# Centroid products as two matmuls in place of three, with the last sum on VectorE

## The chip, the cores and the metric

One core of a Trainium2 chip runs the whole program. The metric is the device time of one execution in microseconds. An execution is timed from outside; the profile's span runs from its first to its last instruction and is a little shorter.

## The reference, cut to what matters

The reference is three layers in a row: attention in which a query sees only the keys of its own cluster, a feed-forward layer with ELU, and a routed layer of eight experts. The change lies in the first. There, for 2 batches x 8 heads, 768 rows and 64 columns:

```
q_n = q / (norm(q) + 1e-06);  k_n likewise;  c_n = centroids / (norm + 1e-06)     # 16 centroids a head
q_assign = argmax(einsum('bhsd,hcd->bhsc', q_n, c_n));  k_assign likewise
mask = q_assign[:, :, :, None] == k_assign[:, :, None, :]
scores = where(mask, q @ k.T / 8, -1e9);  out = softmax(scores) @ v
```

The argmax makes the products with the centroids delicate: two centroids can be nearly as close, so the products are formed in nearly full fp32.

## The kernel before, in words

The attention works through 8 pairs of heads (n = 0 to 7). A pair has 12 units (s = 0 to 11) of 128 queries against 768 keys. A value x that must be exact is held as two fp32r tiles, a head H (x rounded) and a rest L = x - H; a product then is three matmuls, H by H, L by H and H by L.

The steps of a unit are: `scores` (four matmuls of 384 columns into the PSUM tile sA or sB, by turns), `peak` (VectorE takes the row maximum, L402), `exp` (ScalarE, L409), `flip` a and b (six PE transposes, L418, three into the PSUM bank t0 and three into t1), `head` (ScalarE copies a half to ptH, L430), `rest` (VectorE subtracts it to give ptL, L436), `pv` (matmuls with v, L449), and once for two units `pvlow` (ScalarE, L458) and `pvsum` (VectorE, L466). t0 and t1 are one bank each: a flip has to wait until the rest of the flip before it in that bank is done.

Beside these, the next pair is prepared. `similar` (L283, steps simq0, simk0, simq1, simk1, for two halves of 384 tokens) multiplies the centroids with q and k: three matmuls each for q and for k, all six accumulated into partitions 0 to 63 of one PSUM bank, "p". The stationary operand is a window of 64 columns of `cwH` or `cwL`; of its 96 columns only 32 to 63 are not zero, and the window is laid so that q's 32 results land on rows 0 to 31 and k's on rows 32 to 63. `similar_out` (L292, steps sT0 and sT1) copies those 64 rows to SBUF (`rows`) on ScalarE, which frees the bank. `turn_back` (step back) transposes `rows` on the PE, and the steps sv, mx, eqsub, first, least, equal, rows, oT find the argmax and turn it into mask rows. Bank p is used by all steps of this preparation in turn.

Every engine executes its instructions strictly in the order in which the program emits them. That order is written out by hand in `SCHEDULE` (L49), one list for a pair, repeated for each; a plus marks a step for the next pair, a minus one for the pair before. Around the change it reads (L52 to L54, cut):

```
peak2 head0a -head11b -W2 rest0a +simk0 exp2 -W3 -pv5a scores3a +loadqk scores3b +sT0 -rest11b flip1a
peak3 -pv5b flip0b head1a head0b rest1a scores4a exp3 +simq1 rest0b scores4b flip2a peak4 +simk1 head2a vtL
flip1b +sT1 scores5a -pv5c head1b rest2a rest1b exp4 --xH1 scores5b -pv5d --xL1 peak5 loadv flip3a -W4 -W5 -pvlow5 +back
```

Pair 0 is prepared by another list, `START`, ahead of all scores. The constants are built in `first_loads` and `centroids`.

Of the kernel before, what the change touches and what calls it, by code (L numbers as in the profile page):

```python
# [10 lines left out]
F32 = mybir.dt.float32  # L11
F32R = mybir.dt.float32r
# [3 lines left out]
AF = mybir.ActivationFunctionType  # L16
ALU = mybir.AluOpType
# [48 lines left out]
class _Core:  # L66
# [24 lines left out]
    def first_loads(self):  # L91
        nc, c = self.nc, self.const
        V = nc.vector
        cn = self.cn = c.tile([128, 2, 64], F32, name="cn")

        self.load_nat(0, "q")
        nc.scalar.dma_start(out=cn[:, 0, :], in_=self.cent.rearrange("h c d -> (h c) d"))
        self.load_nat(0, "k", nc.scalar)
        self.load_nat(0, "v")
        self.ident = c.tile([128, 128], F32, name="ident")  # L100
        make_identity(nc, self.ident)
        self.ident16 = c.tile([128, 128], BF16, name="ident16")
        V.tensor_copy(self.ident16, self.ident)
        HP = self.H // 2
        self.cwH = c.tile([128, HP, 96], F32R, name="cwH")
        self.cwL = c.tile([128, HP, 96], F32R, name="cwL")
        V.memset(self.cwH.bitcast(F32), 0.0)
        V.memset(self.cwL.bitcast(F32), 0.0)

    def centroids(self):  # L110

        nc, c, cn, HP = self.nc, self.const, self.cn, self.H // 2
        V, S = nc.vector, nc.scalar
        sq = c.tile([128, 64], F32, name="sq")
        V.tensor_tensor(sq, cn[:, 0, :], cn[:, 0, :], ALU.mult)
        t = c.tile([128, 9], F32, name="cnt")
        V.tensor_reduce(t[:, 0:1], sq, axis=AX.X, op=ALU.add)

        S.activation(t[:, 1:2], t[:, 0:1], AF.Sqrt)

        S.activation(t[:, 8:9], t[:, 1:2], AF.Exp, scale=0.0)
        V.tensor_scalar(t[:, 2:3], t[:, 1:2], 1e-30, None, ALU.max)
        V.reciprocal(t[:, 3:4], t[:, 2:3])
        V.tensor_tensor(t[:, 4:5], t[:, 0:1], t[:, 3:4], ALU.mult)
        V.tensor_tensor(t[:, 5:6], t[:, 4:5], t[:, 1:2], ALU.add)
        V.tensor_scalar(t[:, 6:7], t[:, 5:6], 0.5, 1e-6, ALU.mult, ALU.add)
        V.reciprocal(t[:, 7:8], t[:, 6:7])
        V.tensor_scalar(cn[:, 0, :], cn[:, 0, :], t[:, 7:8], None, ALU.mult)
        V.tensor_copy(cn[:, 1, :], cn[:, 0, :])
        pt = self.ps("sA")  # L130
        nc.tensor.transpose(pt[:, 0, 0:128], cn.rearrange("p a d -> p (a d)"), self.ident)
        for j in range(2):
            r = slice(64 * j, 64 * j + 64)
            o = slice(32 + 16 * j, 48 + 16 * j)
            src = pt[r, 0, 0:128].rearrange("p (n j c) -> p n j c", n=HP, j=2)[:, :, j, :]
            V.tensor_copy(self.cwH[r, :, o], src)
            V.tensor_tensor(self.cwL[r, :, o], src, self.cwH[r, :, o].bitcast(F32), ALU.subtract)

    def constants(self):
        nc, c, E = self.nc, self.const, self.E  # L140
# [142 lines left out]
    def similar(self, n, nm, half):  # L283

        p, cs, o = n % (self.H // 2), slice(half * 384, half * 384 + 384), 32 if nm == "q" else 0
        if nm == "q":
            self.sim[n, half] = self.bank_p()
        for j, (w, x) in enumerate(((self.cwH, "H"), (self.cwH, "L"), (self.cwL, "H"))):
            self.nc.tensor.matmul(self.sim[n, half][0:64, 0:384], lhsT=w[:, p, o:o + 64], rhs=self.T[n][nm, x][:, cs],
                                  start=(nm == "q" and j == 0), stop=(nm == "k" and j == 2))  # L290

    def similar_out(self, n, half):  # L292
        self.nc.scalar.activation(self.rows[0:64, half * 384:half * 384 + 384], self.sim.pop((n, half))[0:64, 0:384], AF.Copy)

    def turn_back(self, n):
        ps = self.back[n] = self.bank_p()
# [1087 lines left out]
```

## Time and profile before

| | |
|---|---|
| median of 3 runs | 695.9 us (695.54 to 696.95) |
| profiled execution | 697.57 us, its span 695.8 us |
| mean granted TensorE clock | 0.989 of full speed |
| PE busy | 664.5 us, 96% of the span, 4272 matmuls |
| PEld (weight loads) busy | 606.8 us, 87% |
| VectorE (DVE) busy | 487.7 us, 70% |
| ScalarE (ACT) busy | 448.1 us, 64% |
| GpSimd (POOL) busy | 268.5 us, 39% |

The attention takes about the first third of the span, the feed-forward layer and the experts the rest. Shares of the whole span mix stages with different limits, so the attention has to be read by itself. A pair of heads takes about 30.0 us; step sT0 of the seven pairs after the first starts at 27.26, 57.40, 87.57, 117.56, 147.84, 178.09 and 208.37 us. Busy time counts overlapping instructions once. A PE matmul's duration includes its way through the array; the distance from one start to the next is what it costs in a stream.

### The profile page before, as it was taken

The page shows a single profiled execution, that of the slowest core. Times are in us where ns is not written, and L with a number is a line of the kernel's source. Part 1 is how long each engine was busy: PE and PEld are TensorE (multiplying, and loading weights), DVE is VectorE, ACT ScalarE, POOL GpSimd, SP SyncE. Part 2 cuts the span into 40 slices and gives each one's busy share as a digit, 9 for nine tenths or more (in the row PEclk, how much of TensorE's full clock was granted, in tenths as well). Part 3 has the DMA queues.
Part 4 walks back from the last instruction along what each step waited for, and adds up shares of the span by engine and source line. Part 5 has one row for each costly group of instructions (what it writes and reads, how often), then busy time and mean ns, then how long its engine had stood idle before and what let it go on. Part 6 is the DMA issues. An engine that isn't in the chain of part 4 may idle for free. (4 is left out here: it accounts for less than half of the span.)

```text
span 695.8 us, 12188 instructions
## 1 busy us (share of the span) xinstructions
PE 664.5 (96%) x4272; PEld 606.8 (87%) x4272; DVE 487.7 (70%) x929; ACT 448.1 (64%) x968; POOL 268.5 (39%) x254
## 2 busy tenths in 40 slices
PE   4999999999999988999999999999999998999994
PEld 3799999999998877888888899999999897999994
DVE  5599999999999987999999852432354472226662
ACT  3699989999898986777777664444546321215551
POOL 2323536353455123666788752222242012022010
PEclk9799999999999999999999999999999999999998
DMA  8645757366654623555454355424110259989940
GB/s 175 165 92 130 162 137 163 99 143 140 154 118 118 149 74 107 196 194 192 165 196 161 146 206 210 157 72 145 60 61 16 91 194 374 327 297 315 345 143 13
DMA packets 73670, 111.31 MB, mean 160 GB/s; under 512 B 31073, under 2 KB 41409, under 8 KB 73600
## 3 DMA queue, kind: packets, MB, share of 16 engines
q1 hardware_dynamic: 70400, 106.03, 50.2%
q0 software_dynamic: 1488, 3.99, 1.6%
q8 instruction: 36, 0.59, 0.3%
q10 hardware_dynamic: 1712, 0.43, 0.3%
q14 instruction: 34, 0.28, 0.1%
HBM read 73.81 MB, written 16.92 MB: 130 GB/s over the span
## 5 line engine op out<-in xcount | busy, mean ns | idle before, releaser
L436 DVE TENSOR_TENSOR ptL<-ps_t,ptH 128x384 fp32r<-128x384 f32 x192 | 102.6, 551 | 10.4 <-ACT ptH L430 7.9
L430 ACT ACTIVATE ptH<-ps_t 128x384 fp32r<-128x384 f32 x192 | 91.5, 491 | 17.0 <-PE ps_t L418 13.1
L418 PE MATMUL ps_t<-ident,pe 128*128 128x128 f32 x576 | 94.7, 278 | 2.9 <-DVE ptL L436 2.2
L418 PEld LDWEIGHTS ps_t<-ident,pe 128*128 128x128 f32 x576 | 68.4, 141 | 11.7 <-DVE ptL L436 7.4
L449 PE MATMUL ps_v<-ptH,vt 128*128 128x256 f32 x288 | 78.2, 296 | 0.0
L449 PE MATMUL ps_v<-ptL,vt 128*128 128x256 f32 x288 | 77.2, 296 | 0.0
L697 POOL TENSOR_TENSOR w2L<-r,w2H 128x512 fp32r<-128x512 f32 x28 | 42.4, 1515 | 69.5 <-PE ps_t L742 62.3
L677 POOL TENSOR_TENSOR r<-cv_b,cv_t 128x512 int32<-128x512 int32 x32 | 43.1, 1347 | 44.1 <-DVE cv_b L675 25.5
L449 PEld LDWEIGHTS ps_v<-ptH,vt 128*128 128x128 f32 x288 | 54.0, 189 | 1.6
L449 PEld LDWEIGHTS ps_v<-ptL,vt 128*128 128x128 f32 x288 | 53.5, 190 | 0.2 <-DVE ptL L436 0.2
L725 ACT ACTIVATE e<-ps_p 128x384 f32<-128x384 f32 x32 | 15.7, 491 | 55.4 <-PE ps_p L710 55.4
L402 DVE TENSOR_REDUCE st<-ps_sB 128x1 f32<-128x768 f32 x48 | 45.7, 952 | 4.3 <-PE ps_sB L396 4.2
L402 DVE TENSOR_REDUCE st<-ps_sA 128x1 f32<-128x768 f32 x48 | 45.6, 949 | 4.1 <-PE ps_sA L396 2.9
L1188 POOL DMA_INDIRECT out_dram<-o,dest x10 | 11.5, 1154 | 94.3 <-DVE o L1186 93.7
L728 DVE SCALAR_TENSOR_TENSOR ps_p<-e,ps_p 128x384 f32<-128x384 f32 x32 | 17.9, 559 | 41.1 <-ACT e L726 41.1
L670 DVE SCALAR_TENSOR_TENSOR cv_a<-cv_a,d 128x512 f32<-128x512 f32 x32 | 44.2, 1381 | 3.6 <-ACT cv_a L666 3.4
L697 POOL TENSOR_TENSOR w1L<-r,w1H 128x512 fp32r<-128x512 f32 x32 | 44.1, 1378 | 6.4 <-ACT w1H L696 6.4
L710 PE MATMUL ps_p<-xH,w1H 128*128 128x384 f32 x128 | 44.0, 344 | 2.0 <-DVE gL L731 2.0
L409 ACT ACTIVATE pe<-ps_sA,st 128x768 f32<-128x768 f32 x48 | 43.5, 905 | 0.5 <-DVE st L402 0.5
L409 ACT ACTIVATE pe<-ps_sB,st 128x768 f32<-128x768 f32 x48 | 43.1, 898 | 0.5 <-DVE st L402 0.3
L710 PE MATMUL ps_p<-xL,w1H 128*128 128x384 f32 x128 | 42.9, 335 | 0.0
L710 PE MATMUL ps_v<-xH,w1H 128*128 128x384 f32 x124 | 41.4, 334 | 0.0
(380 smaller groups left out, 1926.3 us busy)
## 6 DMA issues: line engine op xcount, KB each, us to landing
ew<-in_moe_w_dram SPq DMA_DIRECT2D x32, 1024.0 KB
d<-in_moe_w_in_dram SPq DMA_DIRECT2D x16, 512.0 KB
d<-in_moe_w_out_dram SPq DMA_DIRECT2D x16, 512.0 KB
wf_d<-r SPq DMA_DIRECT2D x16, 512.0 KB
r<-wf_d SPq DMA_DIRECT2D x16, 512.0 KB
KA<-kH SPq DMA_DIRECT2D x32, 192.0 KB
natq<-in_q_dram SPq DMA_DIRECT2D x16, 192.0 KB
natv<-in_v_dram SPq DMA_DIRECT2D x16, 192.0 KB
```

What stands on the lines that cost most here:

```text
L402: self.nc.vector.tensor_reduce(st, self.sc[u][:, :, 0:384], axis=AX.XY, op=ALU.max, negate=True)
L409: self.nc.scalar.activation(pe, self.sc.pop(u)[:, :, 0:384], AF.Exp, bias=self.peaks.pop(u), accum_out=self.sums[n][:, s:s + 1])
L418: self.nc.tensor.transpose(ps[:, 0, j * 128:j * 128 + 128], self.pe[u][:, half, j * 128:j * 128 + 128], self.ident)
L430: self.nc.scalar.activation(self.split(u, half)[0], self.tp[u, half][:, 0, 0:384].rearrange("p (c q) -> p c q", c=3), AF.Copy)
L436: self.nc.vector.tensor_tensor(l, self.tp.pop((u, half))[:, 0, 0:384].rearrange("p (c q) -> p c q", c=3), h.bitcast(F32), ALU.subtract)
L449: self.nc.tensor.matmul(self.vp[n, j], lhsT=self.vt[n][:, j // NG, c, :], rhs=t, start=(part == 0 and i == 0), stop=(part == 3 and i == 2 ...
L670: V.scalar_tensor_tensor(a, a, LEAST_HI, hi.bitcast(F32), ALU.is_ge, ALU.mult)
L677: G.tensor_tensor(out.bitcast(I32), b, t, ALU.add)
L697: self.nc.gpsimd.tensor_tensor(l, x, h.bitcast(F32), ALU.subtract)
L710: self.nc.tensor.matmul(ps, lhsT=w[:, c, :], rhs=x[:, c, :], start=(i == 0), stop=(i == 11))
L725: S.activation(e, ps, AF.Relu, scale=-1.0)
L728: V.scalar_tensor_tensor(ps, e, -1.0, ps, ALU.add, ALU.max)
```

## The change

`cwH` and `cwL` become one tile `cw` of 160 columns a pair: the heads in columns 32 to 63, the rests in columns 96 to 127, the others zero. For pairs 1 to 7 the stationary operand is a window of 128 columns, so that one matmul with H and one with L give both parts' products: those with the centroids' heads on partitions 0 to 63, those with the rests on 64 to 127. (The product of the two rests, which was left out before, comes with it.) ScalarE copies partitions 64 to 127 to `rows`, and VectorE adds partitions 0 to 63 from PSUM to them. Pair 0 keeps three matmuls and the single copy.

```diff
-        self.cwH = c.tile([128, HP, 96], F32R, name="cwH")
-        self.cwL = c.tile([128, HP, 96], F32R, name="cwL")
-        V.memset(self.cwH.bitcast(F32), 0.0)
-        V.memset(self.cwL.bitcast(F32), 0.0)
+        self.cw = c.tile([128, HP, 160], F32R, name="cw")
+        V.memset(self.cw.bitcast(F32), 0.0)
...
-            V.tensor_copy(self.cwH[r, :, o], src)
-            V.tensor_tensor(self.cwL[r, :, o], src, self.cwH[r, :, o].bitcast(F32), ALU.subtract)
+            V.tensor_copy(self.cw[r, :, o], src)
+            V.tensor_tensor(self.cw[r, :, 64 + o.start:64 + o.stop], src, self.cw[r, :, o].bitcast(F32), ALU.subtract)
...
-        for j, (w, x) in enumerate(((self.cwH, "H"), (self.cwH, "L"), (self.cwL, "H"))):
-            self.nc.tensor.matmul(self.sim[n, half][0:64, 0:384], lhsT=w[:, p, o:o + 64], rhs=self.T[n][nm, x][:, cs],
-                                  start=(nm == "q" and j == 0), stop=(nm == "k" and j == 2))
+        T, ps = self.T[n], self.sim[n, half]
+        if n == 0:
+            for j, (l, x) in enumerate(((0, "H"), (0, "L"), (64, "H"))):
+                self.nc.tensor.matmul(ps[0:64, 0:384], lhsT=self.cw[:, p, o + l:o + l + 64], rhs=T[nm, x][:, cs],
+                                      start=(nm == "q" and j == 0), stop=(nm == "k" and j == 2))
+            return
+        for x in "HL":
+            self.nc.tensor.matmul(ps[:, 0:384], lhsT=self.cw[:, p, o:o + 128], rhs=T[nm, x][:, cs],
+                                  start=(nm + x == "qH"), stop=(nm + x == "kL"))

     def similar_out(self, n, half):
-        self.nc.scalar.activation(self.rows[0:64, half * 384:half * 384 + 384], self.sim.pop((n, half))[0:64, 0:384], AF.Copy)
+        ps, o = self.sim.pop((n, half)), self.rows[0:64, half * 384:half * 384 + 384]
+        if n == 0:
+            self.nc.scalar.activation(o, ps[0:64, 0:384], AF.Copy)
+        else:
+            self.nc.scalar.activation(o, ps[64:128, 0:384], AF.Copy)
+            self.nc.vector.tensor_tensor(o, ps[0:64, 0:384], o, ALU.add)
```

## Rows read from the trace of the kernel before

**Rows 1.** Windows, one pair: length; busy PE, PEld, DVE, ACT, POOL; PEclk; DMA; GB/s
```profile
147.60:177.60 30.00, 29.88 (x229) 28.07 (x229) 28.02 (x49) 27.52 (x64) 14.12 (x17) 1.00 0.59 136
```

**Rows 2.** The same view, three parts of that pair
```profile
147.80:153.00 5.20, 5.20 (x39) 4.90 (x38) 4.32 (x8) 4.59 (x12) 2.91 (x3) 1.00 0.75 187
153.00:166.00 13.00, 12.88 (x105) 11.84 (x104) 12.79 (x22) 11.54 (x26) 3.02 (x4) 1.00 0.54 130
166.00:178.00 12.00, 12.00 (x91) 11.53 (x90) 11.12 (x21) 11.60 (x27) 8.33 (x12) 1.00 0.59 123
```

**Rows 3.** Timeline of weight loads, 156 to 166 us: those that waited, in brackets for whom
```profile
157.96 0.31 PEld L418 LDWEIGHTS ps_t<-ident,pe 128*128 128x128 f32 x3 [0.44 <-DVE ptL L436]
...
162.03 0.36 PEld L339 LDWEIGHTS <-oh 128*64 128x64 bf16 x6 [0.26 <-DVE oh L333]
```

**Rows 4.** Timeline of PE, 144 to 156 us: start, us, instruction, count
```profile
146.03 0.33 PE L289 MATMUL ps_p<-qL,cwH 128*64 128x384 f32 x1
146.20 0.33 PE L289 MATMUL ps_p<-qH,cwL 128*64 128x384 f32 x1
...
147.24 0.34 PE L396 MATMUL ps_sB<-KA,QA 128*128 128x384 f32 x1
147.42 0.34 PE L396 MATMUL ps_sB<-KB,QB 80*128 80x384 f32 x1
...
148.64 0.49 PE L418 MATMUL ps_t<-ident,pe 128*128 128x128 f32 x3
...
151.04 0.49 PE L418 MATMUL ps_t<-ident,pe 128*128 128x128 f32 x3
```

**Rows 5.** Timeline of PE, 24 to 36 us, first product of pair 1
```profile
25.42 0.52 PE L289 MATMUL ps_p<-qL,cwH 128*64 128x384 f32 x1
25.74 0.52 PE L289 MATMUL ps_p<-qH,cwL 128*64 128x384 f32 x1
```

**Rows 6.** Groups of instructions, 30 to 320 us: count, busy us, mean ns, idle before
```profile
L436 DVE TENSOR_TENSOR ptL<-ps_t,ptH 128x384 fp32r<-128x384 f32 x191 | 102.0, 551 | 10.2 <-ACT ptH L430 7.7
...
L466 DVE TENSOR_TENSOR xr<-ps_v,xtmp 64x256 f32<-64x256 f32 x48 | 20.0, 418 | 3.6 <-ACT xtmp L458 2.4
...
L396 PEld LDWEIGHTS ps_sB<-KA,QA 128*128 128x128 f32 x92 | 17.4, 189 | 0.0
...
L289 PEld LDWEIGHTS ps_p<-kL,cwH 128*64 128x64 f32 x13 | 1.8, 135 | 0.2
```

**Rows 7.** Timeline of ScalarE, 144 to 156 us
```profile
146.96 0.92 ACT L409 ACTIVATE pe<-ps_sA,st 128x768 f32<-128x768 f32 x1
...
147.84 0.48 ACT L293 ACTIVATE rows<-ps_p 64x384 f32<-64x384 f32 x1
...
149.16 0.49 ACT L430 ACTIVATE ptH<-ps_t 128x384 fp32r<-128x384 f32 x1 [0.19 <-PE ps_t L418]
...
150.78 0.49 ACT L430 ACTIVATE ptH<-ps_t 128x384 fp32r<-128x384 f32 x1 [0.24 <-PE ps_t L418]
151.24 0.49 ACT L293 ACTIVATE rows<-ps_p 64x384 f32<-64x384 f32 x1
```

**Rows 8.** Timeline of VectorE, 144 to 156 us
```profile
145.79 0.96 DVE L402 TENSOR_REDUCE st<-ps_sA 128x1 f32<-128x768 f32 x1
146.78 1.02 DVE L436 TENSOR_TENSOR ptL<-ps_t,ptH 128x384 fp32r<-128x384 f32 x2
148.14 0.96 DVE L402 TENSOR_REDUCE st<-ps_sB 128x1 f32<-128x768 f32 x1 [0.34 <-PE ps_sB L396]
149.02 1.23 DVE L436 TENSOR_TENSOR ptL<-ps_t,ptH 128x384 fp32r<-128x384 f32 x2
150.39 0.96 DVE L402 TENSOR_REDUCE st<-ps_sA 128x1 f32<-128x768 f32 x1
151.31 0.56 DVE L436 TENSOR_TENSOR ptL<-ps_t,ptH 128x384 fp32r<-128x384 f32 x1
...
152.64 0.96 DVE L402 TENSOR_REDUCE st<-ps_sB 128x1 f32<-128x768 f32 x1
```

## Prediction

> **What bounds the kernel now.** I read the busy time of each engine by stretch first, taking one pair of heads well inside the attention. PE is busy 29.88 of 30.00 us at the full clock, so PE sets the pace; but VectorE is busy 28.02 and ScalarE 27.52 [rows 1]. Three engines are within 9% of one another, and each waits in order for the others. So the same view in three parts is what decides. From 147.8 to 153, where the products with the centroids lie, PE never rests and VectorE has 0.88 us to spare. From 153 to 166, where the argmax steps lie, VectorE is busy 12.79 of 13.00: here it is the bound. From 166 to 178 PE is full again and VectorE has 0.88 free [rows 2]. The weight loads that waited confirm the middle part: at 157.96 and at 162.03 PE stands still until VectorE has finished [rows 3]. The reader is to see that PE's 100% is an average of two limits: in the middle of each pair nothing can be gained on PE, and whatever comes late on VectorE comes late for all.
>
> **What is removed.** Each half of a pair loses one matmul for q and one for k, four a pair. In a stream one costs the distance from start to start: 146.03 to 146.20, so 0.17 to 0.18 us in rounded rows [rows 4]. That is 0.70 us a pair, 0.35 in each half. In pair 1 the first half runs at half the clock, 0.32 us a matmul [rows 5], so that pair saves 2 x 0.32 + 0.35 = 0.99.
>
> **What gets wider.** Eight weight loads a pair go from 64 to 128 columns: 135 to 189 ns [rows 6]. A 384-column matmul behind a 128-column load starts 147.24, the next 147.42 [rows 4], the same pitch as with 64 columns within 0.01. So I cost the width at nothing; it hides beside the matmul ahead of it. If that cover were gone it would cost 8 x 0.054 = 0.43 a pair.
>
> The Trainium skill speaks against this reading (Trainium Kernel Development and Optimization, Performance Expectations): matmul busy time is called a bad metric, since matmuls are pipelined, and the busy share of weight loads a good one; and TensorE: Matmul & The Clock Gate, section LDWEIGHTS, has a load's time grow with its columns, as the trace does (+54 ns). By that rule PE's limit here would be the loads, 28.07 of 30.00, and the change would relieve PE by only 0.11 us a pair in place of 0.70. The equal pitches don't bear the rule out; it is a rival below.
>
> **What is added.** Two VectorE sums a pair, 64 x 384, one operand in PSUM and one in SBUF. The trace has no such shape. Nearest are the rests, 128x384 with the same operands, 551 ns, and the sums of 64x256, 418 ns [rows 6]. I take 0.55, since the free length is the same, with 0.42 as the lower bound. In a row, one rest after another, each costs 1.02 - 0.55 = 0.47 [rows 8].
>
> **What the sums wait for.** This is the term that decides. VectorE meets the first sum in its order right behind rest0a and ahead of rest11b and peak3, and may not pass it. It needs ScalarE's copy sT0. That copy stands behind exp2, which needs peak2, which VectorE has only just finished. In times: rest0a ends 146.78 + 0.55 = 147.33; exp2 starts at 146.96 and sT0 ends at 147.84 + 0.48 = 148.32 [rows 7, 8]. Neither comes earlier by PE's saving, for ScalarE is bound by its own queue there. From ScalarE's end to VectorE's start passes 0.05 (head0b ends 149.65; rest0b, the second of the two at 149.02, starts 149.70) [rows 7, 8]. So VectorE stands idle from 147.33 to 148.37, 1.04 us, of which only 0.34 was idle before [rows 8].
>
> Walking on with the durations of the rows:
> - sum 148.37; rest11b 148.84 to 149.39, before 147.25 to 147.80: 1.59 late; peak3 149.31, before 148.14: 1.17 late.
> - flip0b overwrites the bank that rest11b reads, so PE can't start it before 149.45. Before it started at 148.64 [rows 4], and with the saved 0.35 could at 148.29: PE stands 1.16 us.
> - From there PE has 2.40 us of work up to flip1b at 151.04 [rows 4], now 0.35 less: flip1b at 151.50, 0.46 late with all four savings spent.
> - head0b moves with flip0b to 149.97, rest0b follows rest1a at 150.66, peak4 starts 151.13, before 150.39.
> - head2a moves 0.81 - 0.17 to 151.42, sT1 behind it to 151.88 and ends at 152.37 [rows 7]. The second sum starts 152.42; VectorE has waited 0.33 since peak4's end.
> - rest2a 152.89, before 151.31; rest1b a pitch later; peak5 153.83, before 152.64: 1.19 late [rows 8].
>
> So VectorE enters its full stretch 1.2 us late, and there only 13.00 - 12.79 = 0.21 can be made up [rows 2]. At 157.96 and 162.03 PE has no slack against it [rows 3], so PE is then 1.0 us late, more than the 0.46 it had. After 166 VectorE can catch up with PE, but PE has nothing to catch up with. Net: +1.0 us a pair, the savings counted.
>
> Bounds for it: VectorE's own sum a pair is 28.02 + 2 x 0.47 + 1.04 + 0.33 = 30.33, so +0.33 at the least unless the waits shrink; with all the idle time it had, less the 0.34 that the first wait covers (1.98 - 0.34 = 1.64), 31.97, so +2.0 at the most. With the 64x256 price the walk gives 2 x 0.13 less, +0.75.
>
> **The sum.** The walk holds for pairs 2 to 7, prepared at 57 to 209 us: 6 x 1.0 = +6.0. Pair 1 saves 0.64 at half clock with VectorE idle beside it, and loses about as much at its second sum: 0, bounds -1.0 and +0.5. One memset in place of two, and the centroids' split, lie at the start beside loads: 0, bounds -0.1 and +0.1. No queue or DMA is moved; bank p is held 0.6 longer, and its next user, simq1, comes after flip0b, which already waits longer. Behind the attention all moves along unchanged. Against the profiled execution 697.57 + 6.0 = 703.6; that execution lies 1.7 above the median shown, so against the runs 695.9 + 6.0 = 701.9.
>
> **Rivals.**
> A: the waits are hidden and the matmuls come through: 6 x -0.70 - 0.99 = -5.2, 690.7. For it: PE is full where they are taken away [rows 2]. It holds if rest11b comes late by less than PE's slack against it, which was 148.64 - 147.80 = 0.84 and is 0.49 after the saving. The walk has 1.59.
> B: VectorE becomes the bound over the whole pair, none of its old idle time being recovered: 6 x 2.0 = +12, 707.9. For it: three engines coupled in order. Against it: its waits for ScalarE and PE after 166 are waits for a PE that would now be ahead.
> C: the lateness is only partly passed on, VectorE making up 0.5 or more in the middle, so that 0 to 0.5 a pair stays: 0 to +3, 695.9 to 698.9. Against it: 0.21 of idle there.
> D: the wide loads set PE's pace. PE saves 0.59 less a pair; half of it, 0.3, falls ahead of sT1 and makes the second sum late: 6 x 1.3 + 0.6 = +8.4, 704.3. Against it: the equal pitches.
> That the change doesn't do what it says I don't count: 28 matmuls fewer is plain from the code.
>
> **How the numbers follow.** About 0.2% (1.4 us) is what a measurement of this kernel can tell from no change. Chances: the walk 0.60 (own range 699 to 706, slower); A 0.13 (0.11 faster, 0.02 same); B 0.08; C 0.16 (half same, half slower); D 0.03. So faster 0.11, same 0.10, slower 0.79. The range 695.5 to 707 takes in the walk, D, C and half of B, and leaves out A and the rest of B, 0.17.
>
> **What would show it.** Right: VectorE waiting about 1 us for ScalarE's copy into `rows` ahead of the first sum in each of six pairs, and about 0.3 ahead of the second; weight loads of the flips waiting for VectorE's rests near 1.2 us once a pair; pairs 31.0 us apart. Wrong: a sum that starts with no wait, a flip0b that follows on PE without a gap, or pairs at 29.3 us (A); pitches over 0.19 in the four matmuls that remain (D); sums far from 0.55 us.

## The result, and the profile after

The changed kernel takes 705.79 us (median of 6 runs, 704.83 to 707.13) against 696.92 before (6 runs, the three shown ahead and three beside the new ones): ratio 1.0127, 95% interval 1.0109 to 1.0145. It is 8.9 us slower; 701.9 was predicted, +6.0. The profiled execution's span is 703.9 us, 8.1 more than before, and its mean granted clock is nearly the same (0.986 and 0.989).

Where the 8.1 us lie is read from the starts of step sT0, one for each pair. The first line is pair 0's copy, the columns are start, duration, instruction:

```profile
11.27 0.48 ACT L301 ACTIVATE rows<-ps_p 64x384 f32<-64x384 f32 x1 [1.43 <-PE ps_p L290]
...
26.36 0.49 ACT L303 ACTIVATE rows<-ps_p 64x384 f32<-64x384 f32 x1
...
57.39 0.49 ACT L303 ACTIVATE rows<-ps_p 64x384 f32<-64x384 f32 x1
...
88.76 0.49 ACT L303 ACTIVATE rows<-ps_p 64x384 f32<-64x384 f32 x1
...
152.00 0.49 ACT L303 ACTIVATE rows<-ps_p 64x384 f32<-64x384 f32 x1
...
183.61 0.49 ACT L303 ACTIVATE rows<-ps_p 64x384 f32<-64x384 f32 x1
```

Before they stood at 11.60, 27.26, 57.40, 87.57, 147.84 and 178.09. Pair 2's step stands where it stood, but this execution came to pair 0's copy 0.33 us earlier; counted from there, pair 1 took 0.32 more. Behind pair 2's step each pair takes 31.56 us on the mean ((183.61 - 57.39) / 4) in place of 30.17 ((178.09 - 57.40) / 4). Six pairs at +1.39 are 8.3.

The windows of one pair, from sT0 to sT0, changed kernel first and kernel before second (length, then busy PE, PEld, DVE, ACT, POOL):

```profile
152.00:183.61 31.61, 29.87 (x228) 28.09 (x227) 28.59 (x50) 28.06 (x63) 14.29 (x18) 1.00 0.57 132
```
```profile
147.84:178.09 30.25, 30.13 (x231) 28.32 (x230) 28.28 (x48) 27.77 (x65) 14.31 (x18) 1.00 0.60 138
```

PE is busy a little less and stands still for 1.74 us where it stood for 0.12. VectorE is busy 0.31 more and stands still for 3.02 in place of 1.97. No engine is full any more: the pair has become a chain of waits. Here is that chain, VectorE first, beside [rows 8]:

```profile
149.80 0.96 DVE L413 TENSOR_REDUCE st<-ps_sA 128x1 f32<-128x768 f32 x1
150.79 0.56 DVE L447 TENSOR_TENSOR ptL<-ps_t,ptH 128x384 fp32r<-128x384 f32 x1
152.51 0.55 DVE L304 TENSOR_TENSOR rows<-ps_p,rows 64x384 f32<-64x384 f32 x1 [1.17 <-ACT rows L303]
152.99 0.54 DVE L447 TENSOR_TENSOR ptL<-ps_t,ptH 128x384 fp32r<-128x384 f32 x1
153.45 0.94 DVE L413 TENSOR_REDUCE st<-ps_sB 128x1 f32<-128x768 f32 x1
154.32 1.00 DVE L447 TENSOR_TENSOR ptL<-ps_t,ptH 128x384 fp32r<-128x384 f32 x2
155.25 0.95 DVE L413 TENSOR_REDUCE st<-ps_sA 128x1 f32<-128x768 f32 x1
156.66 0.55 DVE L304 TENSOR_TENSOR rows<-ps_p,rows 64x384 f32<-64x384 f32 x1 [0.47 <-ACT rows L303]
157.14 1.00 DVE L447 TENSOR_TENSOR ptL<-ps_t,ptH 128x384 fp32r<-128x384 f32 x2
158.07 0.94 DVE L413 TENSOR_REDUCE st<-ps_sB 128x1 f32<-128x768 f32 x1
```

and PE in the same stretch, beside [rows 4]; flip0b has the wait in brackets:

```profile
150.22 0.34 PE L295 MATMUL ps_p<-kH,cw 128*128 128x384 f32 x1
150.39 0.34 PE L295 MATMUL ps_p<-kL,cw 128*128 128x384 f32 x1
...
153.58 0.55 PE L429 MATMUL ps_t<-ident,pe 128*128 128x128 f32 x3 [1.10 <-DVE ptL L447]
...
154.15 0.34 PE L407 MATMUL ps_sA<-KB,QB 80*128 80x384 f32 x1
154.32 0.34 PE L295 MATMUL ps_p<-qH,cw 128*128 128x384 f32 x1
...
157.82 0.52 PE L429 MATMUL ps_t<-ident,pe 128*128 128x128 f32 x3 [0.19 <-DVE ptL L447]
```

The reader is to see the order of cause: the sum waits 1.17 us for ScalarE's copy; rest11b, queued behind it, ends at 153.53; flip0b starts 0.05 later, having cost PE 1.10 us; and the second sum waits again. The matmuls with 128 columns follow one another at the old pitch of 0.17. The sum takes 0.55. Bank p, which the first sum holds longer, delays nothing: the next step that uses it, simq1 at 154.32, starts 0.17 after the matmul ahead of it.

### The profile page after: what moved, and what is told of

It is laid out like the page before. It is cut to its first block, busy times and chain, and to the rows that moved or that the text cites. A ratio compares the mean times of both kernels' runs of the same rounds, so it can differ in the third digit from the quotient of the medians.

```text
span 703.9 us, 12146 instructions
## 1 busy us (share of the span) xinstructions
PE 663.6 (94%) x4244; PEld 606.4 (86%) x4244; DVE 491.1 (70%) x942; ACT 449.8 (64%) x968; POOL 268.3 (38%) x254
```

## The experiments

Each was timed beside the kernel before on the same chip. Between chips the kernel before had medians of 694.3 to 697.0, so ratios are compared, and the length of a pair in the trace (start of sT0 in pair 2 to pair 7, by five): 30.19 us before.

**e1: the sums later.** Same instructions, another place in the order.

```diff
-    peak3 -pv5b flip0b head1a head0b rest1a scores4a exp3 +simq1 rest0b scores4b flip2a peak4 +simk1 head2a vtL
-    flip1b +sT1 scores5a -pv5c head1b rest2a rest1b exp4 ...
+    peak3 +sS0 -pv5b flip0b head1a head0b rest1a scores4a exp3 rest0b scores4b +simq1 flip2a peak4 +simk1 head2a vtL
+    flip1b +sT1 scores5a -pv5c head1b rest2a +sS1 rest1b exp4 ...
     def similar_out(self, n, half):
...
             self.nc.scalar.activation(o, ps[64:128, 0:384], AF.Copy)
-            self.nc.vector.tensor_tensor(o, ps[0:64, 0:384], o, ALU.add)
+            self.late[n, half] = ps, o          # step sS adds them
```

> The two sums stand later in VectorE's order, where ScalarE's copy is already done: the first behind peak3, the second behind rest2a; simq1 moves behind scores4b so that bank p is free. Same instructions as the changed kernel. Theory (the cost is VectorE waiting for ScalarE's copy, 1.17 and 0.47 us a pair): both waits vanish, a pair takes 29.8 to 30.3 us, the time is 695 to 699 us. Rival W (the cost is the work of two more instructions on a nearly full VectorE, wherever they stand): a pair stays above 30.9, 702 to 705 us. Rival S (ScalarE's copy across partitions): unchanged, 705 to 706 us.

Measured: 695.48 us, ratio 0.9984 (0.9974 to 0.9993), pairs of 29.94. Both waits are gone; the sums run back to back with their neighbours:

```profile
146.81 0.96 DVE L418 TENSOR_REDUCE st<-ps_sB 128x1 f32<-128x768 f32 x1
147.69 0.54 DVE L309 TENSOR_TENSOR rows<-ps_p,rows 64x384 f32<-64x384 f32 x1
148.15 1.00 DVE L452 TENSOR_TENSOR ptL<-ps_t,ptH 128x384 fp32r<-128x384 f32 x2
149.08 0.94 DVE L418 TENSOR_REDUCE st<-ps_sA 128x1 f32<-128x768 f32 x1
149.95 0.54 DVE L452 TENSOR_TENSOR ptL<-ps_t,ptH 128x384 fp32r<-128x384 f32 x1
150.43 0.55 DVE L309 TENSOR_TENSOR rows<-ps_p,rows 64x384 f32<-64x384 f32 x1
150.95 0.56 DVE L452 TENSOR_TENSOR ptL<-ps_t,ptH 128x384 fp32r<-128x384 f32 x1
```

So the place of the sums costs 1.6 us a pair (31.56 against 29.94), and the same arithmetic without the waits is a little faster than the kernel before. Rivals W and S, as stated there, fall. The move of simq1 can't be what freed the time, since simq1 did not wait in the changed kernel.

**e2: no sum.** `similar_out` copies `ps[0:64]` and nothing is added.

> Leaves out the products with the centroids' rests: two matmuls, ScalarE copies partitions 0 to 63, no sum. So only PE's saving is left. Theory (VectorE is the bound from the argmax steps on, PE elsewhere): part of the 0.70 us a pair comes through, 0.2 to 0.5, so 693 to 695.5 us. If PE alone set the pace: 0.70 a pair and 0.99 for pair 1, 691.5 us. If wide weight loads set it: no gain, 696 to 697 us.

Measured: 691.31, ratio 0.9936 (0.9916 to 0.9957), pairs of 29.56. The theory's number missed: the saving of PE comes through nearly whole, 0.63 of 0.70 a pair, and 4.5 us in all by the ratio (3.0 to 5.9). The time is the one that was given for PE alone setting the pace. The saving is made ahead of VectorE's full stretch: peak5 starts 6.25 us after peak2 in place of 6.85, and the stretch only passes that on (see the account of the prediction below). The weight loads of this run are still 128 columns wide.

**e3: the third matmul back.**

```diff
             self.nc.tensor.matmul(ps[:, 0:384], lhsT=self.cw[:, p, o:o + 128], rhs=T[nm, x][:, cs], ...
+            if x == "H":
+                self.nc.tensor.matmul(ps[:, 0:384], lhsT=self.zeros, rhs=T[nm, x][:, cs], start=False, stop=False)
```

> The changed kernel with the third matmul put back (it multiplies by zeros), so only the sum's cost is left, without PE's saving. Theory (in the changed kernel the lateness is made by VectorE and ScalarE, PE waits): the first half's matmuls hide in PE's wait ahead of flip0b, one of the second half's lies ahead of the second sum: +0.2 a pair, 706 to 708.5 us. If PE set the pace: +0.70 a pair, 711 us.

Measured: 706.62, ratio 1.0144 (1.0129 to 1.0158), pairs of 31.77. The removed matmuls are worth 0.20 a pair in the changed kernel, as expected, and 0.63 without the sum (e2): PE's saving was mostly eaten by PE's own wait.

**e4: the sum reads no output of ScalarE.** The halves of `cw` are exchanged, and VectorE adds zeros into a tile aside:

```diff
-            self.nc.vector.tensor_tensor(o, ps[0:64, 0:384], o, ALU.add)
+            self.nc.vector.tensor_tensor(t, ps[0:64, 0:384], self.nought, ALU.add)
```

> VectorE's instruction stays where it is, of the same shape, but adds zeros into a tile that nobody reads, so it waits for PE alone; ScalarE's copy still goes from partitions 64 to 127 (which here hold the products with the heads) to 0 to 63. The products with the rests are left out of the result. Theory (the wait for ScalarE is the cost): 696.5 to 700 us, pairs of 30.1 to 30.5. Rival W (the work alone): 703 to 706 us.

Measured: 705.08, ratio 1.0118 (1.0103 to 1.0132), pairs of 31.58. By the number alone the theory falls; the trace says why it does not:

```profile
150.16 0.56 DVE L449 TENSOR_TENSOR ptL<-ps_t,ptH 128x384 fp32r<-128x384 f32 x1
151.88 0.55 DVE L306 TENSOR_TENSOR aside<-ps_p,nought 64x384 f32<-64x384 f32 x1 [1.17 <-ACT rows L304]
```

The wait is still there, with no data passing. All that the two instructions share is bank p, which both read, though on different partitions: this program lets one engine read the bank only after the other. (In e7, where VectorE's instruction does not touch the bank, the wait is gone.) The experiment failed to take the wait away. The Trainium skill (PSUM — Partial Sum Buffer, PSUM bank collisions raise a hardware error) counts reads against reads as collisions, but not in different quadrants of a bank, a quadrant being 32 partitions; no run here tried the latter.

**e7: work at the same place, waiting for nobody.** As e4, with `self.nought` in place of `ps[0:64, 0:384]`.

> As the run e4 (products with the rests left out of the result), but VectorE's instruction adds two SBUF tiles of zeros, 64x384, into a third, so it touches neither bank p nor ScalarE's output and can wait for nobody. In e4 VectorE still waited 1.17 and 0.47 us a pair for ScalarE's copy, which reads the same PSUM bank. Theory (waits of 1.17 and 0.47 a pair make the changed kernel slow): 695 to 699 us. Rival W (the work of two instructions at these places): 703 to 706 us.

Measured: 692.63, ratio 0.9974 (0.9965 to 0.9984), pairs of 29.90. VectorE has two instructions more, at the very places of the changed kernel, and starts them without a wait:

```profile
145.31 0.56 DVE L449 TENSOR_TENSOR ptL<-ps_t,ptH 128x384 fp32r<-128x384 f32 x1
145.78 0.54 DVE L306 TENSOR_TENSOR aside<-nought 64x384 f32<-64x384 f32 x1
146.25 0.54 DVE L449 TENSOR_TENSOR ptL<-ps_t,ptH 128x384 fp32r<-128x384 f32 x1
```

Against the same kernel without them (e5, next) they cost less than 0.1 us a pair. With e1, which makes the whole computation, this settles it: the waits are the cost, the work is not.

**e5: the copy's shift alone.** As e2, with the halves of `cw` exchanged and ScalarE copying `ps[64:128]` to rows 0 to 63.

> As the run e2 (no sum, products with the rests left out), but the products with the heads lie on partitions 64 to 127 and ScalarE's copy moves them to 0 to 63. Told apart: what the shift costs by itself. In the changed kernel the instruction behind such a copy starts 0.51 us after it, in the kernel before 0.38 behind a copy without shift. If ScalarE's place on the path decides: up to 0.25 a pair, 691.5 to 693 us. If ScalarE has room: the same as e2, 691.3.

Measured: 692.13, ratio 0.9967 (0.9955 to 0.9980), pairs of 29.88: 0.32 a pair more than e2, a little above the 0.25 that was expected at the most. One of the five pairs took 30.14, the others 29.64 to 29.87, so the distance from peak2 to peak5 is the better measure: 6.25 in e2, 6.52 in e5, 6.59 in e7. ScalarE's shift costs about 0.3, e7's extra work 0.07 at the most. On ScalarE, e5 first and then e2, second copy of a pair:

```profile
148.35 0.49 ACT L441 ACTIVATE ptH<-ps_t 128x384 fp32r<-128x384 f32 x1
148.86 0.49 ACT L304 ACTIVATE rows<-ps_p 64x384 f32<-64x384 f32 x1
149.37 0.49 ACT L441 ACTIVATE ptH<-ps_t 128x384 fp32r<-128x384 f32 x1
```
```profile
145.97 0.49 ACT L440 ACTIVATE ptH<-ps_t 128x384 fp32r<-128x384 f32 x1
146.36 0.47 ACT L303 ACTIVATE rows<-ps_p 64x384 f32<-64x384 f32 x1
146.73 0.48 ACT L440 ACTIVATE ptH<-ps_t 128x384 fp32r<-128x384 f32 x1
```

Without the shift a copy starts 0.39 after the one ahead of it and the next 0.37 behind it: they overlap by 0.1 us. With it both distances are 0.51.

**e6: the sum on PE.** ScalarE copies all 128 partitions into `both`; for pairs 1 to 7 `turn_back` multiplies instead of transposing (cut):

```diff
-            self.nc.tensor.transpose(ps[:, c * 64:c * 64 + 64], self.rows[0:64, c * 128:c * 128 + 128], ...)
+            self.nc.tensor.matmul(ps[:, c * 64:c * 64 + 64], lhsT=self.both[:, c * 128:c * 128 + 128], rhs=self.twice,
+                                  start=True, stop=True)
```

> Complete computation. ScalarE copies all 128 partitions in one instruction, and the six transposes of turn_back become six fp32 matmuls with two identities on top of one another, so PE makes the sum and VectorE nothing. Theory: like e2 (-0.7 a pair) but for what the six fp32 matmuls cost more than transposes; they are two instructions each in this program's other places. With 0.05 to 0.1 us for each of 12 against 0.5 us for six transposes: +0.1 to +0.7 a pair, so 692 to 696.5 us.

Measured: 694.75, ratio 1.0008 (0.9998 to 1.0018), pairs of 30.22, no difference. The six fp32 matmuls run as twelve, and the next instruction starts 1.29 us after the first of them:

```profile
151.57 1.45 PE L308 MATMUL ps_p<-twice,both 128*128 128x64 f32 x12
152.86 0.27 PE L490 MATMUL ps_p<-ident,sums 128*12 128x128 f32 x1
```

In the changed kernel the six transposes take 0.52:

```profile
158.27 0.58 PE L309 MATMUL ps_p<-ident,rows 64*128 64x64 f32 x6
158.79 0.28 PE L488 MATMUL ps_p<-ident,sums 128*12 128x128 f32 x1
```

That is 0.77 more on PE, and a pair is 0.66 longer than in e2: e2's gain of 0.63 is given back.

**e8 and e9: the operands exchanged.** ScalarE copies `ps[0:64]` in place, VectorE adds `ps[64:128]`; e8 with the sums as late as in e1, e9 with them in place.

> The run e1 with the two operands of the sum exchanged: ScalarE copies partitions 0 to 63 in place, VectorE adds partitions 64 to 127 from PSUM to them. Complete computation. If the shift on ScalarE costs 0.3 a pair (e5 against e2, pairs of 29.88 against 29.56) and VectorE has room for it: pairs of 29.65, about -2 us against e1, ratio to before 0.995. If the shift costs VectorE as much: as e1, 0.998 to 1.000.

> The changed kernel with the operands of the sum exchanged, so that ScalarE's copy has no shift; the sums stay in place and wait. Theory (the waits cost 1.66 a pair, the shift is in them with 0.13 before each copy and 0.13 behind it): pairs of 31.2 to 31.45 in place of 31.56, ratio to before 1.008 to 1.012. If the shift is the main cost: below 1.004.

Measured: e8 695.43, ratio 1.0016 (1.0008 to 1.0025), pairs of 30.35; e9 703.41, ratio 1.0123 (1.0103 to 1.0142), pairs of 31.55. Both expectations missed. e9 is as slow as the changed kernel by the pair, where 31.2 to 31.45 was expected. Against e1, e8 is 0.4 a pair worse, not 0.3 better nor the same: the shift has only changed engines, and it costs more on VectorE. e8's first sum stands like this on VectorE:

```profile
147.46 0.96 DVE L418 TENSOR_REDUCE st<-ps_sB 128x1 f32<-128x768 f32 x1
148.45 0.56 DVE L309 TENSOR_TENSOR rows<-ps_p,rows 64x384 f32<-64x384 f32 x1
149.04 1.02 DVE L452 TENSOR_TENSOR ptL<-ps_t,ptH 128x384 fp32r<-128x384 f32 x2
```

The sum starts 0.99 after peak3 and the rest 0.59 after the sum, where e1 has 0.88 and 0.46. The Trainium skill has this for VectorE (VectorE: DVE Perf Modes, Two Vector instructions with no wait between them): an instruction whose PSUM input starts in another quadrant than the last one's is held until all earlier ones have ended. The trace agrees: the sum and the rest behind it each start 0.03 after the end of the instruction ahead, where in e1 both start 0.08 before it. In e9 the waits ahead of the sums are shorter, 1.01 and 0.32:

```profile
151.52 0.56 DVE L304 TENSOR_TENSOR rows<-ps_p,rows 64x384 f32<-64x384 f32 x1 [1.01 <-ACT rows L303]
152.09 0.56 DVE L447 TENSOR_TENSOR ptL<-ps_t,ptH 128x384 fp32r<-128x384 f32 x1
...
155.64 0.56 DVE L304 TENSOR_TENSOR rows<-ps_p,rows 64x384 f32<-64x384 f32 x1 [0.32 <-ACT rows L303]
156.23 1.02 DVE L447 TENSOR_TENSOR ptL<-ps_t,ptH 128x384 fp32r<-128x384 f32 x2
```

**e10: the first sum later, the second in place.**

> The run e1 with only the first sum moved; the second follows ScalarE's copy at once as in the changed kernel. Tells the two waits apart. By their lengths (1.17 and 0.47): the second keeps 0.3 to 0.7 a pair, pairs of 30.2 to 30.6, ratio 1.001 to 1.005. If the first alone counts: as e1, 0.998. If the second is what reaches the argmax steps late: 1.008 or more.

Measured: 695.60, ratio 1.0016 (1.0006 to 1.0026), pairs of 30.34. The second wait, 0.41 here, is worth 0.40 a pair (against e1), and the first 1.22 (against 31.56), near its length of 1.17.

## Why the prediction was right, and what it mis-sized

**The mechanism held, step by step.** The order was read from the list of steps and the times from the rows: VectorE idle ahead of rest11b, flip0b held by it, a second wait at sT1. The walk had waits of 1.04 and 0.33; measured were 1.17 and 0.47. It had PE standing 1.16 at flip0b; measured 1.10. It had flip0b 1.08 behind the first sum's start (149.45 against 148.37); measured 1.07 (153.58 against 152.51). The time, 705.79, lies at the upper end of the walk's own range of 699 to 706: the path was right, its price too low.

**The mis-sized term is "+1.0 us a pair, the savings counted".** It measured +1.37 (31.56 against 30.19); six of them are +8.2, which is the profile's +8.1. Two parts of the difference are seen. The change was costed as if ScalarE's copy were the same instruction as before; but it now goes from partitions 64 to 127 to partitions 0 to 63 and no longer overlaps its neighbours, which makes each wait 0.13 to 0.14 longer. With the shift taken from ScalarE (e9) the waits are 1.01 and 0.32, the walk's own numbers within 0.03. But e9 is no faster, since VectorE then pays for the shift behind each sum: the rest behind it starts 0.57 and 0.59 after the sum in place of 0.48. So the term lacked a price for the shift, wherever it is put. The other part is the 0.21 that the walk let VectorE make up in its full stretch. Peak5 starts 8.27 after peak2 in place of 6.85, 1.42 late [rows 8]; the walk had 1.19. From peak5 to the next pair's peak2, which stood at 176.04 before and stands at 181.42 now, it is 23.35 in place of 23.40:

```profile
176.04 0.96 DVE L402 TENSOR_REDUCE st<-ps_sA 128x1 f32<-128x768 f32 x1
```
```profile
181.42 0.96 DVE L413 TENSOR_REDUCE st<-ps_sA 128x1 f32<-128x768 f32 x1
```

So only 0.05 was made up. Of the 0.39 a pair that the walk was short (0.98 before rounding), 0.23 was there at peak5 and 0.16 is what was not made up behind it. That second distance hardly moves in any run. A trace has five of them; in the first one 0.2 was made up (23.31 before, 23.11 now), and the others are 23.34 to 23.43 us in the kernel before, the changed kernel and all runs but e6, save for one of e5 (23.61) and one of e9 (23.50). In e6, whose added PE work lies there, they are about 24.0. So nearly all that the change costs or saves is made between peak2 and peak5, and the rest of the pair passes it on.

**"Nothing can be gained on PE" in the middle of the pair** led to a wrong number for e2. The saved matmuls stand ahead of the full stretch; what they save shows at peak5 and is passed on, like what the waits cost.

**The other terms.** The matmuls: 0.70 a pair predicted as PE's saving, 0.63 come through when nothing is added (e2). The width: pitches unchanged, and e2 gains its 0.63 with the wide loads in place; rival D falls. The sum: 0.55 taken from the rests, 0.55 measured. Pair 1: 0 predicted, within -1.0 and +0.5. From pair 0's copy to its own sT0 it saved 0.57, where 0.64 was expected, and to the next sT0 it lost 0.89, so +0.32. That pair 2's step stands within 0.01 of its old place is luck: the execution was 0.33 early at pair 0's copy. Rival A gave 690.7 if the waits were hidden; that is -5.2 us. e2, without sums, has -4.5 by its ratio; e1, with sums that do not wait, has -1.1, and about 0.3 of its 0.38 a pair against e2 is the shift's price in e5. Rival B's +2.0 a pair and C's +0.5 at the most both fall to +1.37.

The best complete version is e1: 0.16% below the kernel before, by the interval 0.07 to 0.26%.

## What to carry to other kernels

In an order written by hand, the price of a new instruction is first where it stands: find what it waits for, what is queued behind it on its engine, and which buffer those hold. Here the same two sums cost 1.6 us a pair more in one place than one or two VectorE instructions later, where they cost about 0.1 (e1 against e5). And work taken off the fullest engine pays only if what replaces it finds a place where its inputs are ready.

## What the runs showed of the hardware that was not expected

- A ScalarE copy whose PSUM input starts at partition 64, with its output and its neighbours at 0, does not overlap them: starts 0.51 apart on both sides, against 0.37 to 0.39, which cost about 0.3 us a pair (e5 against e2). An input that starts at 64 is not needed for it. `pvlow5` of the kernel before reads from partition 0 on and writes from 64 on, and it too starts 0.02 after the end of the instruction ahead and ends 0.02 before the next:

```profile
152.79 0.20 ACT L409 ACTIVATION_READ_ACCUMULATOR pe<-ps_sA,st 128x1 f32 x1
153.01 0.38 ACT L458 ACTIVATE xtmp<-ps_v 64x256 f32<-64x256 f32 x1
153.41 0.49 ACT L430 ACTIVATE ptH<-ps_t 128x384 fp32r<-128x384 f32 x1
```

  Both copies have input and output at different partitions. Whether that decides, or that they differ from their neighbours, was not separated.
- An fp32 matmul of 64 columns runs as two instructions of about 0.11 us each in a stream (1.29 us for twelve), against 0.09 for one of the transposes that it stands for (0.52 for six).
